# Late stores moved from GpSimd's to SyncE's DMA queue, and a different row split of three output tiles, in an attention backward kernel

## Chip, cores and metric

One Trainium2 chip, one core of it. The metric is device time in microseconds (us) of one execution. The kernel before takes 408.85 us (median of 3 runs, 408.64 to 408.96). The profile of one execution covers the span from its first to its last instruction, 406.6 us here.

Engines: PE is TensorE (matmul), DVE VectorE, ACT ScalarE, POOL GpSimd, SP SyncE. GpSimd and SyncE appear here as issuers of DMAs. The DMAs themselves are run by DMA engines, of which the profile's page counts 16.

## The reference, cut to what matters

The program is the forward and the backward pass of a gated sum of a one-token attention over a cache (32 heads, 4096 positions, 128 wide, bf16) and a small MLP. Its inputs and outputs by size:

```
K cache, V cache           2 x 33.5 MB read
dK, dV                     2 x 33.5 MB written   (one outer product a head)
wq (640 x 4096), wo (4096 x 640), w1, w2   read;   their gradients written
ten outputs in all; out_0, out_1 (dx) and out_9 (d gate_w) are 640 numbers each
```

For each head: scores, softmax, output, then `dV = p (x) do`, `dK = ds (x) q`. Nothing is reused between heads, so the kernel is a stream: read 82 MB, write 82 MB.

## The kernel before

All large loads are issued by SyncE and all large stores by GpSimd. Per head one 1 MB tile of K and one of V come in, and one of dV and one of dK go out. These are the parts that the change touches (cuts marked with `...`; `P` = 128 rows, `J*Dh` = 4096 numbers, so a row is 8 KB).

```python
# the stores of dK and dV
def dk_half(h, half):
    ...
    if h == H - 1:                                    # last head: in two halves
        a, b = half * (J // 2), (half + 1) * (J // 2)
        nc.gpsimd.dma_start(dKv[h][:, a:b, :], st["dK"][:, a:b, :])
    elif half == 1:
        nc.gpsimd.dma_start(dKv[h], st["dK"][:])

def dv_half(h, half):
    ...
    if half == 1:
        if h % 10 == 9:                               # heads 9, 19, 29
            spread(dVv[h], st["dV"])
        else:
            nc.gpsimd.dma_start(dVv[h], st["dV"][:])

def spread(dst, t):                                   # 128 rows as 5 + 120 + 3
    src = t[:].rearrange("p j d -> p (j d)")
    out = dst.rearrange("p j d -> p (j d)")
    nc.gpsimd.inc_swdge_sem([], [], mode="reset_dge_cursor")
    for a, b in ((120, 125), (0, 120), (125, 128)):
        nc.gpsimd.dma_start(out[a:b, :], src[a:b, :], max_dma_last_dim=J * Dh)
...
# the gradient of wo, one 640 KB tile a group of four heads
    nc.gpsimd.dma_start(dwo_v[g], wos[g][:])
...
# the gradient of wq: five tiles of 896 KB near the end, and the last columns at the very end
def dwq_store(rc):
    nc.gpsimd.dma_start(dwq_v[:, rc, 0:CL], dwqt[rc][:, 0:CL])
...
nc.gpsimd.dma_start(dwq_v[:, :, CL:], dwq_l[:])       # dwq_l, 640 KB: the last large store
...
# the three small outputs, last of all
for eng, dst, i, cut in ((nc.sync, out0_rows, 0, 4), (nc.scalar, out1_rows, 1, 3), (nc.sync, out9_rows, 2, 2)):
    for a, b in ((0, cut), (cut, RC)):
        eng.dma_start(dst[a:b, :], fin_rows[i * RC + a:i * RC + b, :])
```

Why a tile is stored as 5 + 120 + 3 rows: the cut is meant to give one of the 16 DMA engines, called the spared engine below, fewer rows of this tile than the others. Which engine takes which rows was the author's assumption. A row of such a piece goes as two packets of 4096 B, 159 ns each at the median.

The trace does not name the engine of a packet or of a completion mark (the semaphore of each store counts up sixteen times; each count is called a mark here, and each is read as one engine's, since there are as many). In the kernel before, five of the sixteen marks of head 29's 5-row store come 0.30 to 0.38 us after those of the store before it, the other eleven about 0.2. The latest of the sixteen, at 372.67 us, is one of these five. In the 120-row store that follows, one engine's mark moves by at most 0.57 us and all others, taken in order of time, by 2.3 us or more, and the one that hardly moves is that latest one. So the spared engine has a row of the 5-row piece and little or nothing of the 120-row one. Its number is not shown.

## Time and profile before

| what | value | where it is read |
|---|---|---|
| time | 408.85 us | timed runs |
| moved | 164.93 MB, 406 GB/s | the profile's page |
| last compute, fin_rows | ends 393.4 us | the chain that ended last |
| last store, dwq_l, landed | 401.70 us | the trace's semaphore records |
| SyncE has seen all DMAs | 402.06 us | the trace's instruction records |
| GpSimd's closing drain ends | 405.47 us | the same |
| end of span | 406.56 us | the same |

The closing drain is the DRAIN instruction at the kernel's last line (L852 in the trace), with which each engine ends its part before the closing barrier.

The page of the kernel before, lines of the parts 1 to 3. The DMA row gives, for 40 equal slices of the span, the busy share of the DMA engines in tenths; the row under it what they moved.

```profile
span 406.6 us, 13614 instructions
...
DMA  8999999999999999999999999999999999999991
GB/s 290 420 416 396 422 422 420 419 423 423 421 425 421 422 420 406 424 425 421 422 420 425 424 421 416 410 424 423 425 420 424 424 421 424 422 402 368 406 394 77
DMA packets 27416, 164.93 MB, mean 406 GB/s; under 512 B 3244, under 2 KB 3308, under 8 KB 11484
...
q0 software_dynamic: 12912, 82.03, 49.0%
q1 hardware_dynamic: 14404, 82.03, 48.9%
```

The reader should see that the DMA engines are busy for 80% or more of every slice but the last, so the kernel is bound by them; and that the two queues (q0 is GpSimd's, q1 is SyncE's) share the bytes evenly.

The end of the chain of waits of the kernel before, from 392 us on (start, length, what):

```profile
392.57 0.19 DVE fin_bf L819
392.75 0.04 issue
392.80 0.29 PE fin_ps L821
393.08 0.02 issue
393.11 0.26 ACT fin_rows L823
```

This is a trap. The chain ends with the last instruction of a compute engine, at 393.4 us, 13 us before the span ends. What lies behind it is to be looked for in the DMA and in the closing barrier. The busy time by stretch of the kernel before, whose last two columns are the DMA engines' busy share and GB/s:

```profile
380.00:390.00 10.00, 1.34 (x25) 0.90 (x24) 8.71 (x30) 0.28 (x1) 4.97 (x7) 0.50 1.01 404
390.00:395.00 5.00, 0.27 (x1) 0.09 (x1) 2.57 (x9) 0.26 (x1) 0.00 (x0) 0.50 1.00 395
395.00:400.00 5.00, 0.00 (x0) 0.00 (x0) 0.00 (x0) 0.00 (x0) 0.00 (x0) 0.50 0.59 236
400.00:407.00 7.00, 0.00 (x0) 0.00 (x0) 0.00 (x0) 0.00 (x0) 0.00 (x0) 0.50 0.03 11
```

The compute engines are idle from 395 us on; the DMA engines run dry one after the other between 395 and 402 us (dwq_l's marks come from 395.93 to 401.70); and then there are some 5 us in which nothing moves.

Last, what SyncE waited for after 380 us (in total, times, longest):

```profile
SPq L826 <- ACT fin_rows L823: 56.0, 1, 56.0
SPq L852 <- PEq L852: 4.4, 2, 3.6
SPq L852 <- DMA out_dram<-dwq_l: 4.1, 1, 4.1
SPq L852 <- DMA out_dram<-dK_sb: 1.6, 1, 1.6
```

L852 is the kernel's end. SyncE waits 4.1 us for the last store to land, and then at two closing barriers 4.4 us together, 3.6 us at the first. The view names PE because PE's sequencer takes part in the barrier; which engine came last is told by the records of the trace, read one by one:

```
before: GpSimd's closing drain   387.49 to 405.47     last GpSimd DMA landed 401.70
        SyncE ready for the barrier 402.06            GpSimd answers the barrier 405.51
        second barrier             405.7 to 406.5
```

GpSimd was last: the drains of TensorE, VectorE and ScalarE had ended by 395.1 us. GpSimd's ended 3.77 us after its last DMA had landed, and 3.41 us after SyncE was ready.

### The profile page before, as it was taken

How to read it: one execution, taken by the hardware profiler on the slowest of the kernel's cores; microseconds unless marked ns; L12 is line 12 of the kernel's file. 1: busy time of each engine (PE TensorE's matmuls, PEld its weight loads, DVE VectorE, ACT ScalarE, POOL GpSimd, SP SyncE). 2: the span in 40 equal slices, each digit the busy share in tenths (PEclk: the TensorE clock that was granted, in tenths of full speed). 3: DMA queues.
4: the chain of work that ended last, by engine and by line, in shares of the span. 5: the costliest groups of instructions: out<-in, count | busy, mean ns of one | idle time of the engine just before them, and what ended most of it. 6: DMA issues, size and time to landing. Idle time of an engine off the chain costs nothing.

```text
span 406.6 us, 13614 instructions
## 1 busy us (share of the span) xinstructions
PE 298.3 (73%) x5872; PEld 269.9 (66%) x5872; DVE 303.8 (75%) x791; ACT 177.2 (44%) x411; POOL 55.7 (14%) x105
## 2 busy tenths in 40 slices
PE   0688898678888888478898888458887789859200
PEld 0588787577778777468887877448776778858200
DVE  3338666655899999556689898757999997967860
ACT  1355555344544555225544557315554555434000
POOL 0001111011112111011111113110110121133310
PEclk9999999979998999759998999959999999988655
DMA  8999999999999999999999999999999999999991
GB/s 290 420 416 396 422 422 420 419 423 423 421 425 421 422 420 406 424 425 421 422 420 425 424 421 416 410 424 423 425 420 424 424 421 424 422 402 368 406 394 77
DMA packets 27416, 164.93 MB, mean 406 GB/s; under 512 B 3244, under 2 KB 3308, under 8 KB 11484
## 3 DMA queue, kind: packets, MB, share of 16 engines
q0 software_dynamic: 12912, 82.03, 49.0%
q1 hardware_dynamic: 14404, 82.03, 48.9%
q8 instruction: 46, 0.75, 0.7%
q14 instruction: 14, 0.11, 0.1%
q10 hardware_dynamic: 40, 0.01, 0.0%
HBM read 82.03 MB, written 82.03 MB: 404 GB/s over the span
## 4 chain that ended last, share of the span: by engine, by line
DMA 36%; DVE 33%; PE 19%; ACT 4%; issue 3%; POOL 0%; ACTq 0%; DVEq 0%; POOLq 0%
DMA Kn<-in_A_k_cache_dram 29%; DVE dK_sb L611 8%; PE tr L586 8%; DVE dV_sb L611 7%; DMA out_dram<-dV_sb 6%; DVE junk L382 4%; ACT tT L588 4%; PE sA L665 3%; DVE junk L285 2%; PE sA L595 2%; PE sB L718 2%; DVE junk L534 1%; DVE junk L491 1%; DMA vec_rows<-in_gate_w_dram 1%; DVE dj L705 1%
## 5 line engine op out<-in xcount | busy, mean ns | idle before, releaser
L588 ACT COPY tT<-tr 128x512 f32<-128x512 f32 x256 | 142.3, 588 | 132.6 <-PE tr L586 132.0
L595 PEld LDWEIGHTS <-tT 128*128 128x128 bf16 x2048 | 79.6, 98 | 43.3 <-ACT tT L588 34.2
L586 PE MATMUL tr<-ident_f,Kn 128*128 128x128 f32 x512 | 84.2, 304 | 9.6 <-DMA Kn<-in_A_k_cache_dram 9.6
L611 DVE TENSOR_TENSOR dK_sb<-ds_bf,qd 128x2048 bf16<-128x2048 bf16 x64 | 77.8, 1216 | 3.9 <-DMA out_dram<-dV_sb 3.6
L611 DVE TENSOR_TENSOR dV_sb<-p_bf,qd 128x2048 bf16<-128x2048 bf16 x64 | 78.0, 1218 | 0.6 <-DMA out_dram<-dK_sb 0.3
L586 PE MATMUL tr<-ident_f,Vn 128*128 128x128 f32 x512 | 72.4, 277 | 0.0
L586 PEld LDWEIGHTS tr<-ident_f,Kn 128*128 128x128 f32 x512 | 63.0, 155 | 11.3 <-issue 10.5
L595 PE MATMUL sA<-qd,tT 128*128 128x48 bf16 x1024 | 48.4, 186 | 23.4 <-ACT dq_all L723 12.8
L586 PEld LDWEIGHTS tr<-ident_f,Vn 128*128 128x128 f32 x512 | 55.9, 141 | 0.2
L595 PE MATMUL sB<-qd,tT 128*128 128x48 bf16 x1024 | 46.3, 183 | 0.0
L628 POOL DMA_DIRECT2D out_dram<-dK_sb x31 | 18.4, 594 | 142.8 <-DVE rz L687 93.8
L665 PEld LDWEIGHTS <-Vn 128*128 128x128 bf16 x1024 | 30.6, 96 | 10.3 <-issue 10.3
L641 POOL DMA_DIRECT2D out_dram<-dV_sb x29 | 16.5, 570 | 149.0 <-DVE o_all L710 54.7
L665 PE MATMUL sA<-e_bf,Vn 128*128 128x48 bf16 x1024 | 31.2, 184 | 7.5 <-DVE zs L685 6.2
L718 PE MATMUL sB<-ds_bf,Kn 128*128 128x48 bf16 x1024 | 31.2, 184 | 1.4 <-DVE ds_bf L707 1.4
L669 DVE TENSOR_REDUCE m<-sA 128x1 f32<-128x32 f32 x32 | 6.0, 189 | 34.4 <-PE sA L595 27.8
L718 PEld LDWEIGHTS <-Kn 128*128 128x128 bf16 x1024 | 28.6, 96 | 1.6 <-issue 1.6
L285 DVE SCALAR_TENSOR_TENSOR junk<-wo_g,da_bc 128x640 bf16<-128x640 bf16 x32 | 26.2, 820 | 1.7 <-ACT da_bc L226 1.1
L382 DVE SCALAR_TENSOR_TENSOR junk<-wq_g,dq_bc 128x1024 bf16<-128x1024 bf16 (+1 forms) x25 | 25.1, 1005 | 0.2
L705 DVE TENSOR_SCALAR_CACHE_REDUCE dj<-sB,rz 128x128 f32<-128x128 f32 x32 | 11.1, 346 | 12.8 <-PE sB L699 12.7
L689 ACT ACTIVATE p_bf<-e_bf,rz 128x64 bf16<-128x64 bf16 x32 | 11.1, 348 | 13.6 <-DVE rz L687 10.6
L696 DVE SCALAR_TENSOR_TENSOR pj<-sB,e_bf 128x32 f32<-128x32 f32 x32 | 6.1, 191 | 13.1 <-PE sB L595 12.9
(155 smaller groups left out, 281.0 us busy)
## 6 DMA issues: line engine op xcount, KB each, us to landing
Kn<-in_A_k_cache_dram SPq DMA_DIRECT2D x32, 1024.0 KB, 25.1
Vn<-in_A_v_cache_dram SPq DMA_DIRECT2D x32, 1024.0 KB, 30.0
out_dram<-dK_sb POOLq DMA_DIRECT2D x31, 1024.0 KB, 11.9
out_dram<-dV_sb POOLq DMA_DIRECT2D x29, 1024.0 KB, 11.8
wq_g<-in_A_wq_dram SPq DMA_DIRECT2D x4, 1280.0 KB, 23.0
wo_g<-in_A_wo_dram SPq DMA_DIRECT2D x8, 640.0 KB, 7.3
out_dram<-wo_g POOLq DMA_DIRECT2D x8, 640.0 KB, 12.8
out_dram<-dwq_t POOLq DMA_DIRECT2D x5, 896.0 KB, 13.1
```

Of the source, the lines that this page charges most:

```text
L285: nc.vector.scalar_tensor_tensor(junk[:, 0:D], in0=wos[g][:, i, :], scalar=1.0, in1=da_bc[:], op0=ALU.mult, op1=ALU.mult, accum_out=gp["do ...
L382: nc.vector.scalar_tensor_tensor(junk[:, c0:c1], in0=wqs[w][:, rc, c0:c1], scalar=1.0, in1=dq_bc[:, w * WG * Dh + c0:w * WG * Dh + c1], op ...
L586: nc.tensor.transpose(tp[:, t, :], flat[:, k * P:(k + 1) * P], ident_f[:])
L588: nc.scalar.copy(sb[:].rearrange("p a b -> p (a b)"), tp[:].rearrange("p a b -> p (a b)"))
L595: nc.tensor.matmul(out[:, 2 * k:2 * k + W], lhsT=tb[:, t, par, :], rhs=vec[:, par, :].unsqueeze(1).to_broadcast([P, W // 2, 2]), start=(pa ...
L611: nc.vector.tensor_tensor(dst[:, a:b, :].rearrange("p j (a b) -> p j a b", b=2), col[:, a:b, :].unsqueeze(2).to_broadcast([P, n, Dh // 2, 2]),
L628: nc.gpsimd.dma_start(dKv[h], st["dK"][:])
L641: nc.gpsimd.dma_start(dVv[h], st["dV"][:])
L665: nc.tensor.matmul(O, lhsT=vts[h][:, j, :], rhs=st["e"][:, j:j + 1].to_broadcast([P, W]), start=(j == 0), stop=(j == J - 1))
L689: nc.scalar.activation(p_bf[:], e[:].unsqueeze(2).to_broadcast([P, J, 2]), ACT.Copy, scale=rz[:])
L705: nc.vector.tensor_scalar(dj[:], PT, rz[:], None, ALU.mult, ALU.add, accum_out=dd[:])
L718: nc.tensor.matmul(DQ, lhsT=kts[h][:, j, :], rhs=ds[:, j, 0:1].to_broadcast([P, W]), start=(j == 0), stop=(j == J - 1))
```

## The change

Its intent has two parts. The stores of the last two heads and the other late ones are issued by SyncE, which by then has no loads left to issue. And the three dV tiles that spare one engine are split in a new way, with the `inc_swdge_sem` line before the first tile alone; the author meant the rows that this engine does not take to fall more evenly on the others. In passing, the six small final stores, by SyncE and ScalarE, become three, all by ScalarE. The diff, complete but for context lines:

```diff
+    def ring(h):
+        return nc.sync if h >= H - 2 else nc.gpsimd
@@ dwo
-            nc.gpsimd.dma_start(dwo_v[g], wos[g][:])
+            (nc.sync if g == NG - 1 else nc.gpsimd).dma_start(dwo_v[g], wos[g][:])
@@ dk_half
-            nc.gpsimd.dma_start(dKv[h][:, a:b, :], st["dK"][:, a:b, :])
+            ring(h).dma_start(dKv[h][:, a:b, :], st["dK"][:, a:b, :])
         elif half == 1:
-            nc.gpsimd.dma_start(dKv[h], st["dK"][:])
+            ring(h).dma_start(dKv[h], st["dK"][:])
@@ dv_half
-                spread(dVv[h], st["dV"])
+                spread(h // 10, dVv[h], st["dV"])
             else:
-                nc.gpsimd.dma_start(dVv[h], st["dV"][:])
+                ring(h).dma_start(dVv[h], st["dV"][:])
-    def spread(dst, t):
+    def spread(i, dst, t):
@@ spread
-        nc.gpsimd.inc_swdge_sem([], [], mode="reset_dge_cursor")
-        for a, b in ((120, 125), (0, 120), (125, 128)):
+        if i == 0:
+            nc.gpsimd.inc_swdge_sem([], [], mode="reset_dge_cursor")
+        for a, b in (((120, 125), (0, 120), (125, 128)), ((0, 14), (14, 119), (119, 128)), ((0, 8), (8, 128)))[i]:
@@ dwq_store
-        nc.gpsimd.dma_start(dwq_v[:, rc, 0:CL], dwqt[rc][:, 0:CL])
+        (nc.sync if rc else nc.gpsimd).dma_start(dwq_v[:, rc, 0:CL], dwqt[rc][:, 0:CL])
@@ dwq_l
-    nc.gpsimd.dma_start(dwq_v[:, :, CL:], dwq_l[:])
+    nc.sync.dma_start(dwq_v[:, :, CL:], dwq_l[:])
@@ final rows
-    for eng, dst, i, cut in ((nc.sync, out0_rows, 0, 4), (nc.scalar, out1_rows, 1, 3), (nc.sync, out9_rows, 2, 2)):
-        for a, b in ((0, cut), (cut, RC)):
-            eng.dma_start(dst[a:b, :], fin_rows[i * RC + a:i * RC + b, :])
+    for i, dst in enumerate((out0_rows, out1_rows, out9_rows)):
+        nc.scalar.dma_start(dst, fin_rows[i * RC:(i + 1) * RC, :])
```

## The prediction

> **What bounds it now.** The 16 DMA engines. The page gives 164.93 MB at 406 GB/s over a 406.6 us span; its DMA row reads 8 or 9 in all slices but the last; a packet of 8192 B costs 309 ns in GpSimd's queue and in SyncE's alike. The chain of waits ends with the copy into fin_rows at 393.4 us, but the engines still work off stores: dwq_l, issued at 387.5 us, lands at 401.70, its sixteen completion marks between 395.93 and 401.70. So the slowest engine's total load sets the end of the data. A second tail follows: SyncE has seen every DMA by 402.0 us and then waits 3.6 us at the closing barrier (SyncE's waits), because GpSimd's drain ends only at 405.47, 3.8 us after the last GpSimd DMA landed. The barrier's rest takes 1.1 us.
>
> **What the change does.**
> 1. dK and dV of heads 30 and 31, four of five dwq_t stores, the last wo_g store and dwq_l go to SyncE, which issued its last load at 337.4 us and is free. Issue cost (0.5 to 1.2 us on GpSimd, 0.3 to 0.5 on SyncE) hides behind a backlog of 12 to 14 us. GpSimd's last DMA becomes the first dwq_t store (landed at 379.8), so its drain should end around 384 to 388 us. The 3.4 us from SyncE ready to GpSimd drained should vanish. They lie on the true critical path: the main gain.
> 2. The dV tiles of heads 9, 19, 29. [...] in head 29's 5-row store five of sixteen marks move by 0.30 to 0.37 us, the others by about 0.2. [...] A row costs 0.32 us (estimate: two packets of 159 ns). [...] I take -0.2 us.
> 3. dwq_l by SyncE probably goes in 1024 B packets (GpSimd's went as 4096 B): estimate +0.2 us, from 84 ns for SyncE's 2048 B packets.
> 4. Three final stores for six: inside the tail. Nothing. Compute is untouched.
>
> **Sum.** 408.85 - 3.4 - 0.2 + 0.2 = **405.4 us** (span 403.2), 8 in 10 between 404.0 and 407.0. Faster by over 2%: 0.02; within 2%: 0.96; slower by over 2%: 0.02.
>
> **What would show it.** Right: GpSimd's drain ends before the last landing, SyncE's wait at the closing barrier falls from 3.6 us to well under 1, and the last landing stays within 0.7 us of 401.7. Wrong: the last landing moves by over 1 us, or the drain still ends about 3.8 us after the last DMA of any queue.
>
> **What would make it wrong.** The drain may not depend on GpSimd's own DMAs. SyncE's stores may run at another rate, in a tail that already moves 396 GB/s against 422 before. The slowest engine may be one that gets an extra row. Late stores served from two queues may delay an older store that a buffer waits for; VectorE already waits 3.6 us for one at 361.7 us.

The sum came to 405.4 us: 408.85, less 3.4 for GpSimd's drain, less 0.2 for the new split, plus 0.2 for dwq_l's smaller packets.

## The result

Ratios here and below are from the fast runs of both kernels in the same rounds, so they are not quite the ratio of the medians quoted.

| kernel | median us | range | runs | ratio to before, 95% |
|---|---|---|---|---|
| before | 408.76 | 408.64 to 408.96 | 4 | |
| changed | 404.37 | 404.16 to 405.07 | 4 | 0.9894 (0.9879 to 0.9910) |
| changed again, on another chip | 404.23 | 403.92 to 404.62 | 4 | 0.9879 (0.9862 to 0.9895), before 409.24 |

The change saves 4.4 us, 1.1%: small, but the interval excludes no change. The page of the changed kernel:

```profile
span 402.6 us, 13606 instructions
...
DMA  8999999999999999999999999999999999999995
GB/s 290 420 413 408 422 424 418 419 426 421 423 424 419 395 421 414 421 425 423 423 419 425 425 423 416 412 425 423 421 425 422 424 420 424 424 415 367 413 396 216
DMA packets 27816, 164.93 MB, mean 410 GB/s; under 512 B 3164, under 2 KB 3868, under 8 KB 11884
...
q1 hardware_dynamic: 16480, 91.20, 54.9%
q0 software_dynamic: 11216, 72.85, 43.7%
```

9.2 MB have gone from GpSimd's queue to SyncE's; the bytes and the rate of the full slices are as before. The busy time by stretch at the end of the changed kernel, columns as before:

```profile
380.00:390.00 10.00, 1.63 (x27) 1.10 (x26) 8.71 (x30) 0.37 (x1) 0.00 (x0) 0.50 1.01 415
390.00:395.00 5.00, 0.28 (x1) 0.09 (x1) 2.44 (x9) 0.26 (x1) 0.00 (x0) 0.50 0.86 352
395.00:400.00 5.00, 0.00 (x0) 0.00 (x0) 0.00 (x0) 0.00 (x0) 0.00 (x0) 0.50 0.65 243
400.00:407.00 7.00, 0.00 (x0) 0.00 (x0) 0.00 (x0) 0.00 (x0) 0.00 (x0) 0.66 0.04 13
```

The DMA engines run dry over the same stretch, so the data does not end earlier to speak of. What SyncE waited for after 380 us in the changed kernel:

```profile
SPq L375 <- DMA out_dram<-dV_sb: 4.9, 1, 4.9
SPq L855 <- DMA out_dram<-fin_rows: 4.5, 2, 4.2
...
SPq L855 <- DMA out_dram<-dwq_l: 1.6, 1, 1.6
SPq L855 <- DMA out_dram<-wo_g: 1.1, 1, 1.1
SPq L855 <- PEq L855: 0.7, 2, 0.5
```

The wait at the two closing barriers (L855 is now the kernel's end) is down from 4.4 to 0.7 us. That difference, 3.7 us, is nearly all of the 3.9 us by which these two spans differ. The same records as above, and the sum in full:

```
changed: GpSimd's closing drain   365.42 to 387.05    last GpSimd DMA landed 383.76
         SyncE ready for the barrier 401.88           GpSimd answers the barrier 401.91
         second barrier             402.1 to 402.6

                                        before    changed   saved
last landing                            401.70    401.49    0.21
SyncE ready                             402.06    401.88    0.18
GpSimd answers the first barrier        405.51    401.91    3.60   (3.42 more than SyncE's)
end of span                             406.56    402.64    3.92   (0.32 more: second barrier)
```

The last 0.32 us is not the change's. From GpSimd's answer to the end of the span there are 0.73 or 0.74 us in twelve of the thirteen traces, among them four in which GpSimd is last as well (`split_only`, `before_dwql_sync`, `tail_gpsimd`, `probe`), and 1.05 us in this one trace of the kernel before. What the change takes away is the 3.4 us between SyncE's and GpSimd's readiness.

A new wait has come too, the first line of the SyncE waits: the store of the last wo_g was issued at 391.42 us instead of 386.19, because its semaphore (103 in the trace) was still in use by the store of the last dV, whose last mark came at 391.35 us: the 4.9 us of that line. No cost of it shows: in `late_only` (experiment 1) the same store was issued at 389.06 us, and its last landing was at 401.51 us, against 401.49 here.

SyncE's issues in the changed kernel, from 364 us on (start, length, what):

```profile
370.18 0.35 SPq L644 DMA_DIRECT2D out_dram<-dV_sb  x1
370.58 3.44 SPq L745 DMA_DIRECT2D out_dram<-dwq_t  x2
375.05 0.33 SPq L631 DMA_DIRECT2D out_dram<-dK_sb  x1
379.46 0.33 SPq L644 DMA_DIRECT2D out_dram<-dV_sb  x1
379.85 3.01 SPq L745 DMA_DIRECT2D out_dram<-dwq_t  x2
382.95 3.47 SPq L629 DMA_DIRECT2D out_dram<-dK_sb  x2
391.42 0.33 SPq L375 DMA_DIRECT2D out_dram<-wo_g  x1
393.60 0.38 SPq L791 DMA_DIRECT2D out_dram<-dwq_l  x1
```

The six issues of dwq_t and of the halves of dK, each close behind another, take 1.2 to 2.2 us here (two in 3.0 to 3.5), the others 0.33 to 0.38, and GpSimd's took 0.5 to 1.2. It is not closeness alone: 34 of the 44 SyncE issues before 340 us that began within 0.2 us of the end of another took 0.42 to 0.70 us in this trace. This too hides behind the backlog: these six stores landed 13 us or more after their issue.

### The profile page after: what moved, and what is told of

Its sections match the earlier page's. It is cut to its first block, busy times and chain, and to the rows that moved or that the text cites. A ratio compares the mean times of both kernels' runs of the same rounds, so it can differ in the third digit from the quotient of the medians.

```text
span 402.6 us, 13606 instructions
## 1 busy us (share of the span) xinstructions
PE 300.7 (75%) x5872; PEld 271.9 (68%) x5872; DVE 303.7 (75%) x791; ACT 177.6 (44%) x411; POOL 46.5 (12%) x93
## 4 chain that ended last, share of the span: by engine, by line
DMA 35%; DVE 35%; PE 19%; ACT 4%; issue 3%; POOL 0%; ACTq 0%; SPq 0%; POOLq 0%; DVEq 0%
DMA Kn<-in_A_k_cache_dram 28%; DVE dK_sb L614 9%; PE tr L589 8%; DVE dV_sb L614 7%; DMA out_dram<-dV_sb 6%; DVE junk L385 4%; ACT tT L591 3%; PE sA L669 3%; DVE junk L288 3%; PE sA L598 2%; PE sB L722 2%; DVE junk L537 2%; DVE junk L494 1%; DMA vec_rows<-in_gate_w_dram 1%; DVE dj L709 1%
## 5 line engine op out<-in xcount | busy, mean ns | idle before, releaser
L589 PE MATMUL tr<-ident_f,Kn 128*128 128x128 f32 x512 | 82.8, 300 | 12.8 <-DMA Kn<-in_A_k_cache_dram 12.8
L589 PE MATMUL tr<-ident_f,Vn 128*128 128x128 f32 x512 | 74.3, 281 | 0.0
L589 PEld LDWEIGHTS tr<-ident_f,Kn 128*128 128x128 f32 x512 | 61.9, 153 | 14.2 <-issue 14.2
L589 PEld LDWEIGHTS tr<-ident_f,Vn 128*128 128x128 f32 x512 | 57.3, 144 | 0.0
L631 POOL DMA_DIRECT2D out_dram<-dK_sb x30 | 17.2, 574 | 149.0 <-DVE rz L691 102.2
L722 PE MATMUL sB<-ds_bf,Kn 128*128 128x48 bf16 x1024 | 32.9, 187 | 1.4 <-DVE ds_bf L711 1.4
L722 PEld LDWEIGHTS <-Kn 128*128 128x128 bf16 x1024 | 30.3, 99 | 1.6 <-issue 1.6
L644 POOL DMA_DIRECT2D out_dram<-dV_sb x27 | 14.6, 540 | 136.7 <-DVE o_all L714 48.1
```

The costliest lines, as they stand in the source:

```text
L589: nc.tensor.transpose(tp[:, t, :], flat[:, k * P:(k + 1) * P], ident_f[:])
L631: ring(h).dma_start(dKv[h], st["dK"][:])
L644: ring(h).dma_start(dVv[h], st["dV"][:])
L722: nc.tensor.matmul(DQ, lhsT=kts[h][:, j, :], rhs=ds[:, j, 0:1].to_broadcast([P, W]), start=(j == 0), stop=(j == J - 1))
```

## The experiments

Theory A, of the prediction: GpSimd's closing drain follows the landing of its own last DMA by 3 to 4 us, the closing barrier waits for it, and taking GpSimd's DMAs out of the tail takes that wait away; the new split is worth next to nothing. Rival B: the better balance of the engines gains. Rival C: SyncE's stores move faster. Rival D: the drain's length comes from something else than the landing, such as the amount issued late or a fixed length.

Experiments 1 to 4 ran on one chip, 5 and 6 on a second, 7 to 9 on a third, 10 and 11 on a fourth, each time with the kernel before beside them.

### 1. The late stores alone (`late_only`)

The changed kernel with the old split and the old six final stores.

```diff
-                spread(h // 10, dVv[h], st["dV"])
+                spread(dVv[h], st["dV"])
+    def spread(dst, t):                      # reset, 5 + 120 + 3, as before
...                                           # and the six final stores as before
```

> The late stores by SyncE alone, on the kernel before (old dV splits, old six final stores). Theory A (GpSimd's closing drain follows its last DMA by 3 to 4 us, and that drain was the end of the program): nearly all of the gain, 404.4 to 405.4 us; last landing 401.5 to 402.0 us into the span. Rival B (the better balance of the engines is what gains): 407.5 to 408.8 us. Rival C (SyncE's stores move faster): the last landing comes over 1 us earlier than 401.7.

Measured: 404.84 us (404.29 to 406.12), ratio 0.9899 (0.9879 to 0.9919), before 408.99. Last landing 401.51, drain 366.88 to 387.27, and SyncE's waits after 395 us hold:

```profile
SPq L855 <- PEq L855: 0.6, 2, 0.5
```

This is the whole gain, within the interval, with the data ending as before. Theory A holds; B and C fall, and so does a part of the three final stores in the gain, for this kernel has the old six.

### 2. The new split alone (`split_only`)

```diff
@@ on the kernel before
-                spread(dVv[h], st["dV"])
+                spread(h // 10, dVv[h], st["dV"])
...                                           # the new spread(); all stores stay with GpSimd
```

> The new dV splits alone, on the kernel before. Theory A: 408.2 to 409.0 us, the drain still ends 3.8 us after the last landing and the span about 1.1 us after that; the last landing moves by under 0.7 us. Rival B: 405.5 us or less, from a last landing 3 us earlier.

Measured: 408.56 us (407.81 to 408.82), ratio 0.9983 (0.9965 to 1.0001). The last landing was at 402.25 in the profiled run, not earlier than before's 401.70; the drain ended at 405.98, 3.73 us after it; and SyncE's waits after 395 us hold:

```profile
SPq L853 <- PEq L853: 4.1, 2, 3.6
```

The split moves the time by 0 to 0.35%; whether it does anything is not shown. The wait at the barrier stays.

### 3. One late store given back (`after_dwql_pool`)

```diff
@@ on the changed kernel
-    nc.sync.dma_start(dwq_v[:, :, CL:], dwq_l[:])
+    nc.gpsimd.dma_start(dwq_v[:, :, CL:], dwq_l[:])
```

> The changed kernel with a single late store, dwq_l, given back to GpSimd. Theory A: the whole barrier wait is back: drain about 3.5 us after that store's landing (near 401.5), SyncE waits over 3 us at the barrier, 407.5 to 408.6 us. Rival D (the drain's length depends on how much GpSimd has issued late, or has a fixed length of about 18 to 22 us from its start): the drain begins at once after the issue, so with a fixed length it would end at 405 to 409; if it depends on the amount, little comes back and the time stays under 406 us.

Measured: 405.24 us (404.09 to 405.98), ratio 0.9903 (0.9883 to 0.9922). The number expected of theory A (407.5 to 408.6) was missed by 2.3 to 3.4 us, and the records tell why: GpSimd had no older store under way when this one was issued at 389.22 us (in the changed kernel the others had landed by 383.76), so the store ran beside SyncE's older ones and landed 9.4 us later, at 398.66, before the data's end at 402.21. The drain ended at 401.99, 3.33 us after that landing, and SyncE was ready at 402.65. The mechanism held and its input, the landing time, was guessed wrong: the expectation assumed that the last store issued is the last to land. That held within one queue (before: GpSimd's twenty stores from 341 us on landed in the order of issue), and not between two here.

### 4. One late store taken away (`before_dwql_sync`)

```diff
@@ on the kernel before
-    nc.gpsimd.dma_start(dwq_v[:, :, CL:], dwq_l[:])
+    nc.sync.dma_start(dwq_v[:, :, CL:], dwq_l[:])
```

> The kernel before with dwq_l alone given to SyncE. GpSimd's last DMA is then the wo_g store, which landed at 400.15. Theory A: the drain ends at about 403.9 instead of 405.5, so the time is 406.9 to 407.6 us. Theory D (fixed length from the start): the drain starts about 0.3 us earlier, so the time changes by under 0.5 us. If the engines' queue for the SyncE store lets it pass the older stores, wo_g lands later (up to 401.5) and the gain is under 0.5 us in theory A as well; the landing time of wo_g tells.

Measured: 408.61 us (408.17 to 409.11), ratio 0.9991 (0.9972 to 1.0010): no gain. The expectation's last sentence is what happened: dwq_l, alone in SyncE's queue, shared the engines with GpSimd's stores, so wo_g, now GpSimd's last, landed at 401.45 instead of 400.15. The drain ended at 405.18, 3.73 us after it. Moving only the last store doesn't help; GpSimd must be out of the whole tail.

### 5. A marked store to see the engines (`probe`)

The kernel of experiment 2, with two wo_g stores and one dwq_t store cut into four or five pieces of 2 to 5 rows with different packet sizes, and a rest.

```diff
+    def probe(out, src, parts):
+        nc.gpsimd.inc_swdge_sem([], [], mode="reset_dge_cursor")
+        a = 0
+        for n, size in parts:
+            nc.gpsimd.dma_start(out[a:a + n, :], src[a:a + n, :], **({"max_dma_last_dim": size} if size else {}))
+            a += n
+        nc.gpsimd.dma_start(out[a:P, :], src[a:P, :])
```

> No test of time. The kernel before with the new dV splits, where the last two wo_g stores and the second dwq_t store are cut into pieces of 2 to 5 rows with packets of different sizes, so that the packet sizes tell which engines of the sixteen lag and by how much. [...]

Measured: 415.41 us in its single run (state unknown), and it failed as an instrument. GpSimd's stores take eight semaphores in turn (111 to 118 in the kernel before), and a store waits until the one eight before it has landed (there a dwq_t store on semaphore 118 was issued at 366.92 us, 0.28 us after the dK store eight before it had landed). So many short pieces used these up: the pieces of the first wo_g store were issued at 357.5, 358.3, 362.5, 367.5 and 369.9 us, and the spread of the completion marks, which was to be looked at, fell from 10.1 to 0.24 us, as if the engines had run dry. One reading is of use: the four packets of 1024 B of one piece ran at 364.3, 369.5, 371.1 and 372.5 us, so the packets of one piece can lag differently, by 8.2 us here. On which engines they ran is not shown.

### 6. No split at all (`no_spread`)

```diff
@@ on the changed kernel
-            if h % 10 == 9:
+            if False:
```

> The changed kernel with the three dV tiles stored plainly[...]. [...] if it is then the slowest, the last landing comes 4.5 to 6 us later and the time is 409 to 410.5 us. If the split is worth nothing[...], the time stays within 0.7 us of the changed kernel's 404.4.

Measured: 410.35 us (409.57 to 410.50), ratio 1.0025 (1.0010 to 1.0040), before 408.98. So the split is worth 6 us against the changed kernel's 404.2 to 404.4 (on other chips), within the range that was expected if the spared engine is then the slowest. Cut from the expectation are this engine's number and a count of its rows, from the assumed placement; "it" is this engine. In the last half store of dK fifteen of the sixteen completion marks came between 395.51 and 397.28 us and one at 403.83, 6.55 us after the last of the fifteen; the last landing of all was at 406.94. The stretch after 400 us in this kernel:

```profile
400.00:410.00 10.00, 0.00 (x0) 0.00 (x0) 0.00 (x0) 0.00 (x0) 0.00 (x0) 0.50 0.22 78
```

By this mark one DMA engine ends late, and the author takes it to carry work that the others don't. That it is the spared one is argued from the 6 us that the split gives; its number is not shown. What that work is, the runs don't tell. One candidate stands on the page and was not tested: 46 instruction packets of 16 KB on a queue of their own (q8), 0.7% of the 16 engines' time, so about 1 us of one engine each (an estimate: 0.7% of 16 x 406.6 us over 46); the trace does not say on which engines. GpSimd's drain ended at 394.21 here, far from the end, so this kernel's loss has nothing to do with it. The split as such matters much; what the change did to it is not seen in the time (experiment 2).

### 7. The changed kernel again (`after_again`)

> The changed kernel unaltered, on the same chip as the two below, so that they can be compared. 404.0 to 405.0 us.

Measured: 404.23 us (403.92 to 404.62), last landing 401.44, drain ended at 386.86.

### 8 and 9. Balance taken further (`balance5`, `balance6`)

An attempt at a faster kernel. The sixteen marks of the last dK half store in the changed kernel came between 390.7 and 398.4 us, so some engines end up to 7.7 us before others. From the marks of the cut stores of head 29 (five of which moved by 0.30 to 0.38 us in the 5-row store of the kernel before) and from the assumed placement of rows I took some engines for early and some for late, and searched for cuts that shift rows from the late to the early ones. Which engines these are is not shown.

```diff
@@ on the changed kernel; balance5 (balance6: six tiles of the same kind)
-            if h % 10 == 9:
-                spread(h // 10, dVv[h], st["dV"])
+            if h in CUTS:
+                spread(h, dVv[h], st["dV"])
+    CUTS = {5: (5, 105, 7, 11), 11: (7, 64, 49, 8), 17: (9, 90, 24, 5), 23: (75, 9, 35, 9), 29: (21, 4, 13, 90)}
+        for n in CUTS[h]:
+            nc.gpsimd.dma_start(out[a:a + n, :], src[a:a + n, :], max_dma_last_dim=J * Dh)
+            a += n
```

> The changed kernel with five dV tiles cut (heads 5, 11, 17, 23, 29) instead of three[...]. If the slowest engine's total of rows sets the end of the data[...]: 402.5 to 403.5 us, last landing at about 399.8. If the lag of an engine is not set by its rows, the time stays at 404.0 to 405.0 us; if the early engines become the slow ones, it is over 405 us.

> The same taken further: six dV tiles cut (heads 4, 9, 14, 19, 24, 29)[...]. [...] 401.8 to 403.2 us if rows set the end; over 404 us if the early engines have become the slow ones.

Measured: balance5 406.02 us (404.42 to 406.87), ratio 0.9919 (0.9897 to 0.9941), last landing 402.57; balance6 408.23 us (407.13 to 410.07), ratio 0.9981 (0.9957 to 1.0005), last landing 404.69; the changed kernel on the same chip 404.23. Both are slower, the more so the more rows were moved. That fits rows that set the end and a grouping that was too coarse. It is not a clean test: more pieces also hold up GpSimd's later issues (in balance5 the wo_g store after head 29 goes out at 362.95 us, against 357.47 in the changed kernel), and the two were not separated. In the 21-row piece of head 29 in balance5 seven of the sixteen marks move by about 0.9 us, as for 3 rows each (an estimate, from two packets of 159 ns a row). Two of those seven stood at 368.25 and 368.58, among the three latest of all; in the last dK half store three marks (397.08, 397.34, 399.34) then come over 2 us after the other thirteen. The likely reading, argued from these marks and not tested further, is that two of the engines that were given more rows had not been early, and that the added rows made them the last. No version was found that beats the changed kernel.

### 10 and 11. The same 16 KB store by SyncE and by GpSimd (`tail_sync`, `tail_gpsimd`)

The cleanest test of theory A: one more store, which writes a part of dwq_l again and must therefore wait until dwq_l has landed. The two kernels differ only in who issues it. (The outputs stay right; the bytes are the same.)

```diff
@@ on the changed kernel, as its last line
+    nc.sync.dma_start(dwq_v[0:16, 0, CL:], dwq_l[0:16, 0, :])     # tail_sync
+    nc.gpsimd.dma_start(dwq_v[0:16, 0, CL:], dwq_l[0:16, 0, :])   # tail_gpsimd
```

> The changed kernel with one more store, 16 KB, that writes a part of dwq_l again and therefore is issued after dwq_l has landed; SyncE issues it. Both theories: it lands about 2 us after dwq_l (near 403.5), and the end follows at once: 405.8 to 407.0 us, against the changed kernel's 404.2.

> The same store after the same wait, issued by GpSimd instead. Theory A (GpSimd's closing drain ends 3.1 to 3.8 us after its own last landing and the barrier waits for it): 3 to 4.5 us longer than the SyncE version: 409 to 411 us, SyncE waiting over 3 us at the closing barrier. Rival (the drain takes long only after many or large GpSimd stores, or its length is fixed from its start): within 1.5 us of the SyncE version, or over 415 us if a full 18 to 22 us drain begins after it.

Measured: tail_sync 406.36 us (405.49 to 407.33), ratio 0.9936 (0.9921 to 0.9951); tail_gpsimd 411.87 us (411.50 to 413.16), ratio 1.0076 (1.0062 to 1.0090). The store landed at 403.07 by SyncE and at 403.57 by GpSimd. SyncE's waits after 395 us, of tail_sync:

```profile
SPq L830 <- DMA out_dram<-dwq_l: 5.8, 1, 5.8
...
SPq L856 <- DMA out_dram<-dwq_l: 0.8, 1, 0.8
SPq L856 <- PEq L856: 0.6, 2, 0.5
```

and of tail_gpsimd:

```profile
SPq L856 <- DMA out_dram<-dwq_l: 9.8, 1, 9.8
SPq L856 <- PEq L856: 5.5, 2, 5.0
```

Issued by GpSimd, the same 16 KB cost 5.5 us more, of which 4.9 us are longer waits at the closing barriers (5.5 against 0.6) and 0.5 us is a later landing. The time is above the range that theory A gave (409 to 411 us), as the drain took longer after this landing than after the others.

### The drain over all runs

Read from the instruction records of each trace (us from the span's start):

```
run               drain starts   last GpSimd landing   drain ends   after the landing
no_spread            370.13           391.13             394.21          3.08
after_again          365.44           383.58             386.86          3.28
tail_sync            365.75           383.90             387.18          3.28
changed              365.42           383.76             387.05          3.29
late_only            366.88           383.95             387.27          3.32
after_dwql_pool      389.20           398.66             401.99          3.33
balance5             367.84           385.00             388.69          3.69
split_only           387.68           402.25             405.98          3.73
before_dwql_sync     387.13           401.45             405.18          3.73
before               387.49           401.70             405.47          3.77
balance6             370.28           387.13             390.94          3.81
probe                402.73           408.51             412.77          4.26
tail_gpsimd          401.87           403.57             409.02          5.45
```

The drain's record starts within 0.8 us of GpSimd's last issue in the four traces compared (387.49 against 387.51 us before, 365.42 against 366.20 changed, 389.20 against 389.22 `after_dwql_pool`, 401.87 against 401.89 `tail_gpsimd`), and it ends 3.1 to 3.8 us after that DMA's landing wherever the landing came at least 9 us after the start. Its own length runs from 7.2 to 24 us, so a fixed length is ruled out, and a single 16 KB store is enough for it, so the amount is not what makes it. In the two runs where the landing came soon after the start (5.8 and 1.7 us) it ends later after it, by 4.3 and 5.5 us. What the drain does in that time is not shown.

## Why the prediction was right, point by point

- **What bounds the kernel.** Right: the DMA row stays full, and the last landing moved only from 401.70 to 401.49 us, within the 0.7 us that the prediction allowed.
- **The closing barrier (-3.4 us).** Right in mechanism and size: SyncE's waits at the barriers fell from 4.4 to 0.7 us, the drain ended at 387.05 (384 to 388 was said), before the last landing, and GpSimd's answer came 3.42 us nearer to SyncE's. `late_only` gives the whole gain without the split, and the pair of tail stores shows that it is the issuer that matters. The rest of the barrier, taken as unchanged at 1.1 us, was read from the one trace in which it is 1.05; all others have 0.73 or 0.74, with GpSimd last or not.
- **The rest of the 1 us.** The prediction said 405.4 us and 404.37 was measured. Of that, 0.2 us is the earlier end of the data and 0.3 us the long second barrier of the one trace of the kernel before. The other 0.5 us is not in the traces: the profiled runs differ by 3.9 us in both span and time (408.38 to 404.50), the medians by 4.4. Single runs of one kernel differ by as much. So about 0.8 us of the 4.4 has no cause that is shown.
- **The split (-0.2 us).** Not shown: 0.9983, interval 0.9965 to 1.0001. What is shown is that one engine is spared, by the marks of the 120-row stores (0.57 us at most against 2.3 or more, before), and that the split as such is worth 6 us (experiment 6). The rows an engine behind the -0.2 were the author's assumption and are not shown. This -0.2 and the +0.2 of the next point cancel in the sum, so the total tests neither.
- **dwq_l in small packets (+0.2 us).** The packets are as said: 640 of 1024 B at 46 ns in SyncE's queue, against 160 of 4096 B at 159 ns in GpSimd's; shared evenly by 16 engines (an estimate) 1.84 us an engine against 1.6. No later end was seen for it.
- **Issue cost 0.3 to 0.5 us on SyncE.** Wrong: up to 2.2 us for one of the late stores, and 4.9 us of waiting for a semaphore. It was off the path, as the prediction said of issue cost as such.
- **Late stores served from two queues.** Named as a risk; it did reorder landings (experiments 3 and 4), but in the changed kernel no buffer wait came of it that showed in the time.

## What to carry to other kernels

When a kernel ends with a stream of stores, look past the chain of waits at the closing barrier: here, stores issued last from GpSimd cost GpSimd's drain, which ended 3.1 to 5.5 us after their landing, and cost nothing that showed when GpSimd's last DMA landed 3.6 us before the data's end (experiment 3). Move the whole late group and not only the last store: in experiment 4 the two queues shared the engines, and the store left with GpSimd landed 1.3 us later. And where rows are shifted between DMA engines to balance them, first measure each engine's lag: experiment 5 shows the four packets of one piece up to 8.2 us apart, and the traces here name no engine.
